# Sixteen rows of one V tile in layers two and four, moved from SP's queue to GpSimd's queue

## The chip, the cores and the metric

The kernel runs on one core of a Trainium2 chip. The metric is the device time of one launch in microseconds (us); the figure given for a version is the median of several runs. A profile of one execution, taken by the hardware profiler, goes with it. In what follows PE is the matrix engine (TensorE), DVE is VectorE, ACT is ScalarE, POOL is GpSimd, and SP is the engine that does little but issue DMAs. The core has 16 DMA engines, which do all transfers between HBM and the on-chip memory SBUF.

## The reference, cut to what matters

Four decode steps of attention, one token, one after the other; layers one and three use the weights and caches A, layers two and four B.

```python
def attention(x, k_cache, v_cache, wq, wo):        # x [1, 1, 640], caches [1, 32, 8192, 192]
    q = (x @ wq).reshape(1, 1, 32, 192).transpose(0, 2, 1, 3)
    scores = einsum("bhqd,bhkd->bhqk", q, k_cache) * 192 ** -0.5
    o = einsum("bhqk,bhkd->bhqd", softmax(scores), v_cache)
    return o.transpose(0, 2, 1, 3).reshape(1, 1, 32 * 192) @ wo

x = x + attention(layernorm(x), A_k, A_v, A_wq, A_wo)
x = x + attention(layernorm(x), B_k, B_v, B_wq, B_wo)
x = x + attention(layernorm(x), A_k, A_v, A_wq, A_wo)
x = x + attention(layernorm(x), B_k, B_v, B_wq, B_wo)
```

Everything is bf16. K and V of one layer are 2 x 32 x 8192 x 192 elements, so nearly all of the work is reading caches: the page of the profile counts 848 MB read in one launch.

## The kernel before

**Tiles.** The 32 heads are taken in 16 pairs. The K cache of a pair is one tile of 128 partitions: 64 partitions for each head, 128 keys of 192 elements on each, 49,152 bytes a partition. V of a pair has the same form. SBUF holds a `pool` of eight slots of half a tile (24,576 bytes a partition) each; a whole tile takes two neighbouring slots.

**One pair.** `products` (from line 589) multiplies K by the query on DVE in four chunks a half (line 599) and sums over the head dimension on PE with an identity matrix (lines 58 and 612). `softmax` takes maxima and exponentials. `values` (from line 641) multiplies the probabilities by V on PE (lines 58 and 678) and `gather` picks the two heads' results out of the accumulator (lines 696 and 697). At the end of a layer the last pair's results are projected by `wo` and give the next layer's input.

**Order of the work.** The program is written out by hand into one list of instructions for each engine (class `Queue`), with semaphores between them. `plan` is the list of transfers in the order in which SP issues them; `steps` is the order of the computation. `allot` gives each transfer of the plan its slots, and `before` names the tenants of those slots that must be done first. `transfer` (line 345) appends one DMA to SP's list behind waits for those tenants (`free`); `ahead` (line 404) appends as many as have known tenants. All 182 large transfers, the weights' too, go through SP's one queue, and each engine of the 16 takes its share of every transfer in that order. A tile whose halves are loaded together (`whole`) is one DMA of 128 rows of 49,152 bytes (line 379). Its completion adds 16 to the semaphore of its first slot, and `values` makes PE wait for that semaphore (line 664) before the first of its matmuls.

**Who else loads.** ACT issues one transfer, the 1.2 KB input `x` (line 420). The engines' own instructions come from HBM too, in pages, on queues of their own. POOL writes a few constants at the start and then does one small instruction in each layer (line 461, a power for the layer norm); it issues no DMA.

**Layers.** Layers one and two use index `l` 0 and 1, layers three and four 2 and 3; `p` counts the pairs of a layer in the order in which they are taken. The twelfth pair is `p` 11. Of the V tiles, pairs 14 and 15 of layer two stay in SBUF for layer four.

Of the kernel before, what the change touches and what calls it, by code (L numbers as in the profile page):

```python
# [7 lines left out]
BF16 = mybir.dt.bfloat16  # L8
# [53 lines left out]


PAIRS_W = 5
NSLOT = 8
KEPT = {0: {("k", 0)}, 1: {("v", 14), ("v", 15)}}


def build(nc, A_x, A_k, A_v, A_wq, A_wo, B_x, B_k, B_v, B_wq, B_wo, out):
    _, H, SK, DH = A_k.shape  # L70
    D = A_x.shape[-1]
    P = 128
# [9 lines left out]
    PD = 2 * DH  # L82
    NW = PAIRS_W * PD // P
    QC = (NPAIR - 1) * PD
    QR = QC // 3
    TS = JU * DH
# [5 lines left out]
    VK = 8  # L92
    FORWARD = dict(pairs=list(range(NPAIR)), q0=0, q1=1, wo=[0, PAIRS_W, 2 * PAIRS_W], wol=NPAIR - 1)
    BACKWARD = dict(pairs=[15, 14, 11, 12, 13] + list(range(1, 11)) + [0], q0=NPAIR - 1, q1=0,
                    wo=[NPAIR - PAIRS_W, 1, 1 + PAIRS_W], wol=0)
    ORDER = [FORWARD, FORWARD, FORWARD, BACKWARD]

    with ExitStack() as ctx:
        def sb(name, shape, dt):
            return ctx.enter_context(nc.sbuf_tensor(name, shape, dt))  # L100
# [4 lines left out]
        def sem(name):  # L105
            return ctx.enter_context(nc.semaphore(name))

        ident = sb("ident", [P, P], BF16)
        pool = sb("pool", [P, NSLOT * TS], BF16)
# [36 lines left out]
        xb = sb("xb", [P, DC], BF16)  # L146
        zero = sb("zero", [P, 33], BF16)
        part = [sb(f"part{i}", [P, DC], BF16) for i in range(3)]

        QM = ps("QM")  # L150
        SP_ = [ps("S0"), ps("S1")]
# [15 lines left out]
        PE = Queue(sem("pPE"))  # L167
        DV = Queue(sem("pDVE"))
        AC = Queue(sem("pACT"))
        PO = Queue(sem("pPOOL"))  # L170
        SP = Queue()
        semS = [sem(f"semS{i}") for i in range(NSLOT)]
        semOL, semOE, semOB, semVQ, semX, semOUT = [sem(n) for n in ("semOL", "semOE", "semOB", "semVQ", "semX", "semOUT")]

        e = PO.op(lambda g: g.memset(ident[:], 0.0))
        PO.op(lambda g: g.affine_select(out=ident[:], in_=ident[:], compare_op=ALU.not_equal, fill=1.0,
# [33 lines left out]
        def whole(kind, l, p):  # L210
# [3 lines left out]
            if kind == "k":  # L214
                return l < 2 and p not in (PAIRS_W, 2 * PAIRS_W) or l == 3 and p > 1
            if p == NPAIR - 1:
                return False
            return l != 2 or p not in (0, PAIRS_W, 2 * PAIRS_W)

# [6 lines left out]
        for l in range(NL):  # L226
# [8 lines left out]
            for p in range(NPAIR):  # L235
# [17 lines left out]
                if p < NPAIR - 2:  # L253
                    if first_load("v", l, p) == (l, p):
                        plan += [("v", l, p, u) for u in range(2)]
                        if l == 2 and p == 1:
                            i = plan.index(("k", l, 1, 0))
# [70 lines left out]
                    plan[i:i + 2] = [m, n]  # L328
                    turn[n[1:3]] = (1, 0)

        freed, landed = {}, {}
        issued = [0]

        def wq_rows(l, g):
# [10 lines left out]
        def transfer(n):  # L345
            l = n[1]
            o = ORDER[l]
            w = W[l % 2]
            free = [freed[b] for b in before[n]]
            if n[0] in ("wol", "woe"):  # L350
                r0 = o["wol"] * PD
                a, b = (0, OI) if l < 3 else (0, OI - 1) if n[0] == "wol" else (OI - 1, OI)
                return SP.op(lambda s: s.dma_start(
                    rows[:, a * D:b * D], w["wo"][r0:r0 + PD].rearrange("(p i) n -> p (i n)", p=P)[:, a * D:b * D]),
                    *free, sem=semOL if n[0] == "wol" else semOE, inc=16)
            if n[0] == "t":
                return max(free, key=lambda e: e[1]) if free else None
            if n[0] == "wob":
                r0 = o["wo"][2] * PD
                return SP.op(lambda s: s.dma_start(  # L360
                    slot[place[("wo", l, 2)]][:, (NW - NB[l]) * D:NW * D],
                    w["wo"][r0:r0 + PAIRS_W * PD].rearrange("(p i) n -> p (i n)", p=P)[:, (NW - NB[l]) * D:]),
                    sem=semOB, inc=16)
            if n[0] == "vq":
                n = ("v", l, NPAIR - 1, 1)
            i = place[n]
            t = slot[i]
            if n[0] in "kv":
                h = 2 * pair(l, n[2])
                r = w[n[0]][0, h:h + 2].rearrange("h (p j) d -> (h p) (j d)", j=J)  # L370
                if quarters(n):
                    x = TS // 2
                    if n in landed:
                        return SP.op(lambda s: s.dma_start(t[:, x:], r[:, TS + x:]), sem=semVQ, inc=16)
                    return SP.op(lambda s: s.dma_start(t[:, 0:x], r[:, TS:TS + x]), *free, sem=semS[i], inc=16)
                if whole(*n[:3]):
                    if n[3] == 1:
                        return landed[n[:3] + (0,)]
                    f = lambda s: s.dma_start(pool[:, i * TS:(i + 2) * TS], r)
                else:  # L380
                    f = lambda s: s.dma_start(t, r[:, n[3] * TS:(n[3] + 1) * TS])
            elif n[0] == "wq" and l < 2:
                f = lambda s: s.dma_start(pool[:, i * TS:i * TS + DC * QW], w["wq"].rearrange("(p c) n -> p (c n)", c=DC))
            elif n[0] == "wq":
                c0, k = Q_PARTS[n[2]]
                f = lambda s: s.dma_start(
                    wq_rows(l, n[2]),
                    w["wq"][:, o["q1"] * PD:o["q1"] * PD + QC].rearrange("(p c) n -> p c n", c=DC)[:, c0:c0 + k, :])
            else:
                r0 = o["wo"][n[2]] * PD  # L390
                k = NW - NB[l] if n[2] == 2 else NW
                f = lambda s: s.dma_start(
                    t[:, 0:k * D], w["wo"][r0:r0 + PAIRS_W * PD].rearrange("(p i) n -> p (i n)", p=P)[:, 0:k * D])
            return SP.op(f, *free, sem=semS[i], inc=16)

        def need(n):

            while n not in landed:
                m = plan[issued[0]]
                issued[0] += 1  # L400
                landed[m] = transfer(m)
            return landed[n]
# [45 lines left out]
        def layer(l, ev_z, ev_true):  # L448
# [192 lines left out]
            def values(p, us=(0, 1)):  # L641

                par = (l * NPAIR + p) % 2
                nl, np_ = first_load("v", l, p)
                k = 2 if p == NPAIR - 1 else VK
                N = min(512, k * DH)
                PE.wait(ev_p[p])
                if 0 in us:
                    PE.wait(last["rl"])
                    if p < NPAIR - 1:  # L650
                        e = PE.op(lambda t: t.matmul(TB[96:97, C_L:C_L + 2], lhsT=ones[:, 0:1], rhs=l_col[par][:],  # L651
                                                     start=True, stop=True), bank=TBu)
                    else:
                        for h in range(2):
                            e = PE.op(lambda t, h=h: t.matmul(TB[64 * h:64 * h + 64, C_L:C_L + 1], lhsT=ones[:, 0:1].broadcast_to([P, 64]),
                                                              rhs=l_col[par][:, h:h + 1], start=True, stop=True),
                                      signal=h == 1, bank=TBu)
                    last["lc"][par] = ev_l[p] = e
                PE.wait(last["O"])
                rounds = J // k // G  # L660
                for r in range(us[0] * rounds // 2, (us[-1] + 1) * rounds // 2):
                    u, i = divmod(r, rounds // 2)
                    u = turn[nl, np_][u]
                    PE.wait(need(("v", nl, np_, u)))
                    t = slot[place[("v", nl, np_, u)]]
                    if p == NPAIR - 1 and i == rounds // 4 and quarters(("v", nl, np_, u)):
                        if l == 3:
                            busy(6)
                        PE.wait(need(("vq", l)))
                    for c in range(k * DH // N):  # L670
                        for g in range(G):
                            j = (i * G + g) * k
                            o, x, y = (O[32 * g:32 * g + 2 * k, c * N:(c + 1) * N],
                                       p_sb[par][:, u * JU + j:u * JU + j + k, :].rearrange("p j h -> p (j h)"),
                                       t[:, j * DH + c * N:j * DH + (c + 1) * N])
                            f, fin = r == 0, r == rounds - 1
                            e = PE.op(lambda t, c=c, g=g, o=o, x=x, y=y, f=f, fin=fin: (
                                t.matmul(o, lhsT=x, rhs=y, start=f, stop=fin) if c == 0 else  # L678
                                matmul_held(t, o, x, y, f, fin, 32, 32 * g)),
                                signal=(fin and c == k * DH // N - 1 and g == G - 1), bank=Ou)  # L680
                if 1 not in us:
                    return
                ev_O[p] = last["p"][par] = e
                if not stays("v", l, p):
                    for u in range(2):
                        freed[("v", nl, np_, u)] = e
# [80 lines left out]
            if l + 1 == NL:  # L767
                a = slot[place[("wo", 3, 2)]][0:33, 0:HD]
# [63 lines left out]
```

## Time and profile before

| | us |
|---|---|
| median of 3 runs | 1982.47 |
| lowest, highest | 1982.34, 1984.11 |
| the profiled execution: first to last instruction (its span) | 1982.1 |

No other time is listed for the profiled execution. Its span is 0.4 us under the median, which is the launch around the span and the difference between executions.

| | |
|---|---|
| bytes read from HBM | 848.36 MB |
| mean rate over the span | 428 GB/s |
| busy: PE, DVE, ACT, POOL | 65%, 61%, 7%, under 1% |
| twelfth V tile of layer two: issued by SP, landed | 855.92, 888.5 |
| the same of layer four | 1809.76, 1855.1 |

The times of the last two rows are from the span's start. The trace records, besides the instructions, every packet that the DMA engines moved (its queue, start, duration and size, but not which engine moved it) and the time of each of the 16 steps by which a transfer's completion raises its semaphore, one for each DMA engine. One row of a K or V tile is one packet. Where such records are used, the text says so; everything else is on the page of the profile or in its views of waits, chain and timeline.

### The profile page before, as it was taken

The numbers are of one execution on the slowest core, as the hardware profiler recorded it, in microseconds if no ns is written. First come the engines' busy times: TensorE is split into PE (matmuls) and PEld (weight loads), VectorE is DVE, ScalarE is ACT, GpSimd is POOL, SyncE is SP. The second block draws the span as 40 slices with busy tenths as digits, with TensorE's granted clock in tenths as the row PEclk, the third lists the DMA queues.
The fourth block names the chain that finished last, engine by engine and source line by source line (L and its number), as shares of the span: only waits on it lengthen the run. The fifth ranks groups of instructions, "written<-read, shape, count | busy, mean of one in ns | idle before, by whom it ended". The sixth has DMA issues, their size and how long they took to land.

```text
span 1982.1 us, 13748 instructions
## 1 busy us (share of the span) xinstructions
PE 1288.6 (65%) x8248; PEld 146.4 (7%) x3160; DVE 1201.2 (61%) x1376; ACT 139.9 (7%) x462; POOL 4.5 (0%) x23
## 2 busy tenths in 40 slices
PE   3567476666466666666785676675776766657658
PEld 0001001000100100100020010010001001000001
DVE  3566467467166657556745565665764775665656
ACT  0000000000000000000010000000000100000000
POOL 0000000000000000000000000000000000000000
PEclk9787776778677777777887877878787888777779
DMA  9999999999999999999999999999999999999998
GB/s 414 438 431 430 431 436 432 430 430 429 435 432 433 434 430 432 429 435 433 426 407 426 425 426 426 432 430 431 434 429 427 435 431 433 433 432 431 433 433 367
DMA packets 26930, 849.25 MB, mean 428 GB/s; under 512 B 3058, under 2 KB 3188, under 8 KB 3828
## 3 DMA queue, kind: packets, MB, share of 16 engines
q1 hardware_dynamic: 26724, 848.38, 99.6%
q8 instruction: 45, 0.74, 0.2%
q14 instruction: 17, 0.14, 0.0%
q10 hardware_dynamic: 144, 0.00, 0.0%
HBM read 848.36 MB, written 0.00 MB: 428 GB/s over the span
## 4 chain that ended last, share of the span: by engine, by line
DMA 67%; DVE 17%; PE 15%; ACT 1%; issue 0%; SPq 0%
DMA pool<-in_B_k_cache_dram 27%; DMA pool<-in_A_v_cache_dram 20%; DVE pool L599 15%; DMA pool<-in_A_k_cache_dram 14%; PE S L58 6%; DMA pool<-in_B_v_cache_dram 6%; PE OY L58 5%; PE OY L678 3%; DVE acc L697 1%; ACT p_sb L636 1%; DVE s_sb L621 1%; PE S L612 0%; DVE m_bf L623 0%; PE OY L538 0%; PE QM L626 0%
## 5 line engine op out<-in xcount | busy, mean ns | idle before, releaser
L599 DVE TENSOR_TENSOR pool<-pool,q_sb 128x3072 bf16<-128x3072 bf16 x512 | 861.1, 1753 | 229.5 <-DMA pool<-in_B_k_cache_dram 133.5
L58 PE MATMUL S<-pool,ident 128*128 128x512 bf16 x2944 | 789.5, 425 | 19.5 <-DVE pool L599 17.6
L710 PE MATMUL TB<-acc,small 128*1 128x192 f32 x240 | 82.7, 495 | 212.0 <-DVE acc L697 212.0
L58 PE MATMUL OY<-pool,p_sb 128*16 128x512 bf16 x1920 | 202.7, 498 | 0.0
L696 DVE TENSOR_SCALAR acc<-OY,small 128x192 f32<-128x192 f32 x64 | 26.7, 418 | 287.5 <-PE OY L58 256.3
L678 PE MATMUL OY<-pool,p_sb 128*16 128x512 bf16 (+1 forms) x1216 | 148.2, 495 | 69.5 <-DMA pool<-in_A_v_cache_dram 63.5
L612 PE MATMUL S<-pool,ident 128*128 128x512 bf16 x128 | 61.8, 483 | 201.3 <-DVE pool L599 201.2
L697 DVE SCALAR_TENSOR_TENSOR acc<-OY,small,acc 128x192 f32<-128x192 f32 x424 | 177.1, 418 | 14.9
L621 DVE TENSOR_REDUCE s_sb<-S 128x64 f32<-128x512 f32 x128 | 88.0, 688 | 69.7 <-PE S L58 69.7
L527 ACT ACTIVATE q_sb<-QM 128x192 bf16<-128x192 f32 x60 | 19.9, 331 | 944.0 <-PE QM L521 944.0
L721 ACT ACTIVATE rows<-TB,small 1x192 bf16<-1x192 f32 x120 | 43.2, 406 | 596.3 <-PE TB L710 596.3
L692 DVE RECIPROCAL small<-TB 1x2 f32<-1x2 f32 x64 | 11.2, 175 | 94.5 <-PE TB L651 75.3
L636 ACT ACTIVATE p_sb<-s_sb,small 64x128 bf16<-64x128 f32 x128 | 55.7, 435 | 161.2 <-DVE small L630 160.4
L612 PEld LDWEIGHTS S<-pool,ident 128*128 128x128 bf16 x128 | 12.9, 101 | 676.2 <-DVE pool L599 604.4
L651 PE MATMUL TB<-small,ones 128*1 128x2 f32 x120 | 11.4, 165 | 74.1 <-ACT p_sb L636 74.1
L678 PEld LDWEIGHTS OY<-pool,p_sb 128*16 128x16 bf16 (+1 forms) x1216 | 39.8, 107 | 217.3 <-issue 138.8
L626 PE MATMUL QM<-ident,m_bf 128*64 128x64 bf16 x128 | 14.0, 216 | 54.4 <-DVE m_bf L623 53.9
L710 PEld LDWEIGHTS TB<-acc,small 128*1 128x1 f32 x240 | 19.8, 101 | 310.8 <-DVE acc L697 284.0
L630 DVE TENSOR_REDUCE small<-QM 128x1 f32<-128x64 f32 x64 | 14.4, 225 | 35.2 <-PE QM L626 35.2
L521 PEld LDWEIGHTS QM<-rows,one_b 1*64 1x64 bf16 x120 | 6.2, 100 | 347.0 <-issue 341.1
L538 PE MATMUL OY<-oT,pool 128*128 128x1 bf16 x675 | 28.6, 178 | 1.9 <-ACT oT L584 1.9
L538 PEld LDWEIGHTS OY<-oT,pool 128*128 128x128 bf16 x675 | 27.8, 131 | 3.8 <-ACT oT L584 2.5
(74 smaller groups left out, 215.2 us busy)
## 6 DMA issues: line engine op xcount, KB each, us to landing
pool<-in_B_k_cache_dram SPq DMA_DIRECT2D x28, 6144.0 KB, 37.9
pool<-in_B_v_cache_dram SPq DMA_DIRECT2D x28, 6144.0 KB, 33.5
pool<-in_A_v_cache_dram SPq DMA_DIRECT2D x27, 6144.0 KB, 27.5
pool<-in_A_k_cache_dram SPq DMA_DIRECT2D x34, 3072.0 KB, 20.5
pool<-in_A_k_cache_dram SPq DMA_DIRECT2D x14, 6144.0 KB, 36.4
pool<-in_A_v_cache_dram SPq DMA_DIRECT2D x10, 3072.0 KB, 14.7
pool<-in_B_k_cache_dram SPq DMA_DIRECT2D x8, 3072.0 KB, 22.5
pool<-in_A_wo_dram SPq DMA_DIRECT2D x6, 2400.0 KB, 21.9
```

The source lines that it names most:

```text
L58: return t.add_instruction(mybir.InstMatmult(name=t.bass.get_next_instruction_name(), engine=mybir.EngineType.PE, ins=[t.lower_ap(rhs), t. ...
L527: lambda a: a.activation(q_sb[i][:], QM[:, 0:DH], ACT.Copy), e, last["q"][i], bank=QMu)
L538: e = PE.op(lambda t, i=i, c=c, f=y_first[0], fin=n[0] == "wol" and i == k - 1: t.matmul(YB[:, c:c + 1], lhsT=t3[:, i, c:D:DC], rhs=o[:, i ...
L599: e = DV.op(lambda v, d0=d0: v.tensor_tensor(k3[:, :, d0:d0 + QD], kin[:, :, d0:d0 + QD], q_sb[qi][:, d0:d0 + QD].unsqueeze(1).broadcast_t ...
L612: t.matmul(S[:, :], lhsT=ident[:], rhs=k3[:, :, d0:d0 + R], start=True, stop=fin) if d0 == 0 else
L621: lambda v, u=u: v.tensor_reduce(s[:, u * JU:(u + 1) * JU], SP_[u][:].rearrange("p (j r) -> p j r", r=R), AX.X, ALU.add), ev_S[p, u], last ...
L636: ev_p[p] = AC.op(lambda a, h=h, r=r: a.activation(p_sb[par][r, :, h], s[r, :], ACT.Exp, bias=negm[par][r, 0:1], accum_out=l_col[par][r, h ...
L678: t.matmul(o, lhsT=x, rhs=y, start=f, stop=fin) if c == 0 else
L696: v.tensor_scalar(acc[:], O[:, 0:DH], pick[:, 0:1], None, ALU.mult) if i == 0 else
L697: v.scalar_tensor_tensor(out=acc[:], in0=O[:, i * DH:(i + 1) * DH], scalar=pick[:, i:i + 1], in1=acc[:], op0=ALU.mult, op1=ALU.add)), e if ...
L710: e = PE.op(lambda t, h=h: t.matmul(TB[96:97, C_O + h * DH:C_O + (h + 1) * DH], lhsT=half[:, h:h + 1], rhs=acc[:], start=True, stop=True), ...
L721: last["TO"] = last["row_written"] = AC.op(lambda a, h=h: a.activation(orow[:, o0 + h * DH:o0 + (h + 1) * DH], TB[96:97, C_O + h * DH:C_O ...
```

## The change

The V tile of the twelfth pair in layers two and four (`("v", 1, 11)` and `("v", 3, 11)`) comes in five transfers in place of one. SP issues the first 112 rows. POOL issues the last 16 in two transfers of eight rows, 112 to 119 and 120 to 127. Ahead of each of these it issues a transfer of the first two elements of the same eight rows (4 bytes a row) into a tile `turned` that nothing reads. All four wait, on POOL, for the same tenants as SP's transfer, and add 16 each to a new semaphore `semA`. PE waits for `semA` as well as for the slot's semaphore before the first matmul of that tile. The lists of DVE and ACT are as before; SP's has the same transfers in the same order, two of them with 112 rows in place of 128; POOL's gains eight DMAs, four behind its second small instruction (the one of layer two) and four behind its last.

```diff
+ASIDE = {("v", 1, 11), ("v", 3, 11)}
+ASIDE_ROWS = 16
...
+        turned = sb("turned", [P, 2], BF16)
...
-        freed, landed = {}, {}
+        freed, landed, aside = {}, {}, {}
...
                 if whole(*n[:3]):
                     if n[3] == 1:
                         return landed[n[:3] + (0,)]
-                    f = lambda s: s.dma_start(pool[:, i * TS:(i + 2) * TS], r)
+                    if n[:3] in ASIDE:
+                        for a in range(P - ASIDE_ROWS, P, 8):
+                            PO.op(lambda g, a=a: g.dma_start(turned[a:a + 8], r[a:a + 8, 0:2]), *free, sem=semA, inc=16)
+                            aside[n[:3]] = PO.op(lambda g, a=a: g.dma_start(pool[a:a + 8, i * TS:(i + 2) * TS], r[a:a + 8]),
+                                                 *free, sem=semA, inc=16)
+                        a = P - ASIDE_ROWS
+                        f = lambda s: s.dma_start(pool[0:a, i * TS:(i + 2) * TS], r[0:a])
+                    else:
+                        f = lambda s: s.dma_start(pool[:, i * TS:(i + 2) * TS], r)
...
-                    PE.wait(need(("v", nl, np_, u)))
+                    PE.wait(need(("v", nl, np_, u)), aside.get(("v", nl, np_)))
```

More of the change, by code (lines that the diff above doesn't have):

```diff
@@ L172, in build @@
         semS = [sem(f"semS{i}") for i in range(NSLOT)]
-        semOL, semOE, semOB, semVQ, semX, semOUT = [sem(n) for n in ("semOL", "semOE", "semOB", "semVQ", "semX", "semOUT")]
+        semOL, semOE, semOB, semVQ, semX, semOUT, semA = [
+            sem(n) for n in ("semOL", "semOE", "semOB", "semVQ", "semX", "semOUT", "semA")]
         e = PO.op(lambda g: g.memset(ident[:], 0.0))
```

## The prediction

> **What bounds the kernel now.** I read the slices first, then the table of queues.
>
> ```profile
> DMA  9999999999999999999999999999999999999998
> GB/s 414 438 431 430 431 436 432 430 430 429 435 432 433 434 430 432 429 435 433 426 407 426 425 426 426 432 430 431 434 429 427 435 431 433 433 432 431 433 433 367
> ...
> q1 hardware_dynamic: 26724, 848.38, 99.6%
> q8 instruction: 45, 0.74, 0.2%
> q14 instruction: 17, 0.14, 0.0%
> q10 hardware_dynamic: 144, 0.00, 0.0%
> ```
>
> The DMA engines are full in every slice; only the 21st (the change to layer three, 407) and the last (367) fall off. So the time is bytes over rate, and a gain or loss must come from how evenly the 16 engines are loaded. The page gives only their mean. The packet records give more: a row of 49,152 bytes takes 1.815 us, and each engine starts the next at once. Chaining packets (the one that starts where another ended) gives sixteen unbroken chains, one an engine. They start within 1.1 us of one another and drift apart. The 16 completion steps say the same: they lie 1.1 us apart for the first transfer and 6.35 us for layer two's last V transfer.
>
> What drives the drift is the other queues. Each 16,384-byte instruction page (q8) puts one engine back by 1.55 us, and these pages go round exactly eight engines in turn. Each 8,192-byte page of one kind (q14) puts back a ninth engine, always the same, by 0.97 us, six times before the end of layer two. The other seven are hardly hit. Lag behind the first engine:
>
> - end of layer two: seven at 0 to 1.82 us, the eight page engines at 2.95 to 5.67, the ninth at 6.35;
> - end of layer four: seven at 0 to 2.25, the eight at 3.18 to 6.18, the ninth at 5.36.
>
> The chain of work that ended last shows that the slowest engine is the one that counts, and at just these two ends:
>
> ```profile
> 993.05 16.54 DMA pool<-in_B_v_cache_dram
> 1009.62 1.48 PE OY L678 x14
> ...
> 1937.43 37.95 DMA pool<-in_B_v_cache_dram
> 1975.43 0.85 PE OY L678 x16
> ```
>
> PE starts on the layer's last V piece 0.04 us after it has landed whole. In between the queue never runs dry, so the lags are carried on; at the change to layer three the fast engines do run dry (the spread falls to 2.4 us), so layer two's lag is paid, and layer four starts its own.
>
> **The change, part by part.**
>
> *SP's transfers.* Two of 128 rows become 112: seven rows an engine in place of eight, if all 16 share evenly as in every transfer of the trace. Each engine is relieved of 1.815 us a layer.
>
> *POOL's eight-row transfers.* A row is one packet in all K and V transfers shown, so eight rows reach at most eight engines. Each transfer has a small one of the same row count ahead of it; if the seats are given out in turn, small ones sit on one eight and large ones on the other, both times. Then eight engines carry 7 + 2 = 9 rows (1.82 us more than before) and eight carry 7 (1.82 less). No row of this trace shows which eight. But there are nine late engines and eight seats, and the nine are split: whichever eight is loaded, somebody late is in it.
>
> - If the loaded eight are those without q8 pages, they hold the ninth engine: layer two ends at 6.35 + 1.82 = 8.17 (+1.82), layer four at 5.36 + 1.82 = 7.18 against 6.18 (+1.00). Sum +2.8.
> - If the loaded eight are the page engines: 5.67 + 1.82 = 7.49 against 6.35 (+1.14), and 6.18 + 1.82 = 8.00 (+1.82). Sum +3.0.
> - The best eight (the seven quick ones and the least late): 2.95 + 1.82 = 4.77 against 6.35 (-1.58), 3.18 + 1.82 = 5.00 against 6.18 (-1.18). Sum -2.8.
>
> I take the mean of the first two, +2.9, because the pages' eight look like a half of the engines, as the seats would be; the third needs a set drawn for this purpose.
>
> [...]
>
> *Cost of a second queue beside the first.* No POOL DMA is in the trace. The nearest rows: the 10-byte packets of ACT's one transfer (q10) put the rows beside them back by nothing that shows; a 16,384-byte page costs 1.55 us, where its size at a row's rate is 0.60, so 0.95 too much; an 8,192-byte page 0.97 against 0.30, so 0.67. Between 0 and 0.95 I take 0.5 a large packet, near the middle, since a row is data like q1's but its queue is software-fed like neither. Two packets a loaded engine and layer: 4 x 0.5 = +2.0 (0 to 3.8). Nothing excludes that it is below that of q1's own rows, but an engine that is never idle has nothing to win.
>
> *The small transfers and completions.* Eight packets of 4 bytes each, and 16 completion steps for each of four transfers. Completion packets on q1 take 9 ns: 4 x 9 ns is nothing. From above, the smallest page's 0.67 for each of four on every engine: 2.7 a layer, 5.4 in all. I take 0, the nearer in size.
>
> *POOL's list.* Four waits and four issues a layer. Behind the first four stands line 461 of layer three, and for that there is time:
>
> ```profile
> 855.92 0.33 SPq L379 DMA_DIRECT2D pool<-in_B_v_cache_dram  x1
> ...
> 1016.75 0.55 POOL L461 TENSOR_TENSOR small<-small 128x1 f32<-128x1 f32 x1 [501.41 <-DVE small L460]
> ```
>
> POOL waits for the same tenants as SP, so it is let go by 855.92 and has 160 us before its next instruction. Nothing stands behind the second four. Price: 0; if POOL were late there, ACT's scaling of the query waits for it.
>
> *PE's added wait.* Behind it stands PE's whole list: the V products, then the next pair's sums. SP's part of the tile lands at 888.5, 32.6 us after its issue, because some 18 us of other transfers (32.6 less its own 8 x 1.815) are ahead of it on q1; in layer four it is 45 us. POOL's rows have their own queue and need two rows' time, 2 x 1.815, or twice that when they alternate with q1's. Even behind the whole backlog they come with SP's rows. Price: 0; if they took longer, each us past 888.5 + 3.2 (PE takes the tile up at 891.7) is a us of PE, of which the backlog on q1 hides the first 18.
>
> *SP and DVE, ACT.* SP issues the same number of DMAs (0.33 us each); DVE and ACT have the same lists. 0.
>
> **The sum.** Span 1982.1 + 2.9 + 2.0 = 1987.0, and 0.4 around it (median of the runs less the span): **1987.4**. This case alone reaches from 1982.1 + 0.4 + 2.8 = 1985.3 to 1982.5 + 3.0 + 3.8 + 5.4 = 1994.7.
>
> **The rivals.**
>
> 1. *The balance improves.* The seats fall on the quick engines and relieve the late ones: -2.8, and with no second-queue cost 1979.7. For it: the spread of 6.35 us is real, and the mean of the lags at the two ends is some 3 us, so there is something to win. Against it: nine late for eight seats. It decides from the point where the loaded eight hold at most one late engine.
> 2. *The change doesn't move the load.* If the two large transfers sit on different eights, every engine carries 7 + 1 = 8 rows as before, and only a second-queue packet remains, one an engine and layer: 2 x 0.5 = +1.0, so 1983.5. Speaks for it that nothing shows the seats' order.
> 3. *The rows of the side transfers hinder one another.* Eight neighbouring partitions are filled by eight engines at once, which no transfer of the trace does. From above: one after the other, 8 x 1.815 = 14.5 us a transfer, 29.0 a layer against the 3.6 in my sum, so +25 a layer, up to 2038. It counts only as far as a loaded engine's q1 rows stand still meanwhile; a page shows that they do, the row beside it takes 0.48 us longer on top of the page's 1.07. Against it: every row of the trace took 1.82 with 16 engines writing at once. I put it at a third of that, 2004.
>
> [...]
>
> **How the numbers follow.** My forecast's case has 0.52, rival 1 0.09, rival 2 0.14, rival 3 0.20, and 0.05 is for what I don't see (POOL's transfers late). The range runs from rival 1 (1979.5) to the end of the forecast's case (1995) and leaves out rival 3 and little else. A measurement of this kernel can tell about 0.2% from no change, 4.0 us: below 1978.5, above 1986.4. Faster beyond that: 0.04, since the balance can't give it. Slower: rival 3, three fifths of the forecast's case, most of the unseen: 0.57. Within: 0.39.
>
> **What would show it.** On the page: two new queues' worth of packets beside q1, 32 rows fewer on q1. In the completion steps of layer two's last V transfer: a spread of over 7.5 us shows the load on late engines, under 5 rival 1, about 6.5 rival 2, over 12 rival 3. The side rows' own packets: about 1.8 us each, or 4 and more for rival 3. The forecast is wrong if the loaded eight are the quick ones, if the side rows take much longer than q1's, or if PE waits for `semA` where it waited for the slot (line 664 of before).

## The result

The changed kernel took **2055.32 us** (median of 4 runs, 2053.57 to 2059.34), the kernel before 1982.4 on the same chip (4 runs, 1981.95 to 1984.11). The ratio is 1.037, with a 95% interval of 1.0356 to 1.0384: 72.9 us slower, against 5 foretold and a range that ended at 1995. The profiled execution took 2055.56, its span is 2053.7.

**The profile after.** The slices and the table of queues, from the page:

```profile
DMA  9999999999999999999999999999999999999998
GB/s 414 433 435 431 430 430 433 435 429 430 434 430 432 430 436 428 376 213 428 425 392 430 427 429 433 434 417 436 426 427 436 430 431 434 435 430 254 333 433 340
...
q1 hardware_dynamic: 26692, 846.80, 98.8%
q0 software_dynamic: 256, 1.57, 0.6%
q8 instruction: 45, 0.74, 0.1%
```

The two rows must be read together. The first still says 9 in every slice but the last, as before; the second falls to 213 GB/s in the 18th slice and to 254 in the 37th. These are the places of the two changed tiles. The DMA engines were busy there, but at half the rate: a packet that is held up counts as busy (below, from 870 to 885 us, a share of 1.03 at 206 GB/s). POOL's q0 moved 1.57 MB, 0.2% of the bytes.

The same stretch of layer two in windows, after and then before (columns: stretch, its length, the busy time and count of PE, PE's weight loads, DVE, ACT and POOL, the PE clock, the DMA share, GB/s):

```profile
850.00:870.00 20.00, 12.87 (x84) 1.25 (x27) 7.11 (x15) 1.31 (x5) 2.24 (x4) 0.79 1.14 335
870.00:885.00 15.00, 0.00 (x0) 0.00 (x0) 0.00 (x0) 0.72 (x2) 0.00 (x0) 0.50 1.03 206
885.00:925.00 40.00, 14.63 (x66) 0.68 (x16) 15.42 (x13) 1.31 (x5) 0.00 (x0) 0.63 0.93 208
925.00:945.00 20.00, 10.60 (x63) 0.82 (x17) 9.98 (x12) 0.72 (x2) 0.00 (x0) 0.62 1.00 433
```

```profile
850.00:870.00 20.00, 13.02 (x86) 1.22 (x27) 7.06 (x15) 1.54 (x6) 0.00 (x0) 0.80 1.00 431
870.00:885.00 15.00, 8.97 (x34) 0.20 (x2) 10.95 (x7) 0.49 (x2) 0.00 (x0) 0.70 1.00 433
885.00:925.00 40.00, 26.15 (x176) 2.13 (x50) 24.57 (x32) 3.34 (x12) 0.00 (x0) 0.83 1.00 432
925.00:945.00 20.00, 12.03 (x45) 0.54 (x6) 14.83 (x13) 0.72 (x2) 0.00 (x0) 0.74 1.01 435
```

From 870 to 925 the rate is 206 to 208; before, the same four stretches had 431 to 435. From 870 to 885 PE and DVE do nothing at all: they have run out of tiles. The rate comes back at once after the tile (433 from 925 to 945).

How long the transfers took (columns: tile, engine that issues, count, KB of each, median us from issue to landing), the two kinds of the change, and the whole V tiles of B before:

```profile
pool<-in_B_v_cache_dram SPq DMA_DIRECT2D x2, 5376.0 KB, 76.4
...
pool<-in_B_v_cache_dram POOLq DMA_DIRECT2D x4, 384.0 KB, 28.4
```

```profile
pool<-in_B_v_cache_dram SPq DMA_DIRECT2D x28, 6144.0 KB, 33.5
```

SP's 112 rows needed 76.4 us (such a tile of 128 rows before: 33.5), POOL's eight rows 28.4. The chain of work that ended last, in the places that the prediction showed and in the one where the time went:

```profile
850.42 48.39 DMA pool<-in_B_k_cache_dram
...
916.64 7.42 another core or an unknown queue
...
1021.83 15.84 DMA pool<-in_B_v_cache_dram
...
2009.17 37.75 DMA pool<-in_B_v_cache_dram
```

The K tile issued at 850.42, just ahead of the changed V tile, already took 48.4 us. Before, the same tile was issued at 850.79 and by its completion steps had landed at 874.0, after 23.2 us, so rows of a transfer that was not changed are slow too. At 916.64 PE waits 7.42 us for the changed tile. The view cannot name the queue. The completion steps can: `semA` had its last step at 898.5 us from the span's start, and SP's 112 rows theirs at 924.06, where PE's wait ends. So PE waited for SP's rows, not for POOL's. The pieces at 1021.83 and 2009.17 stand at the ends of layers two and four. The second is the same last V piece as before, 37.75 us against 37.95. The first is the half tile just ahead of layer two's last two V pieces, 15.84 us; before, the chain went through the last of these, 16.54. They are no longer than the pieces before; they start later. By the completion steps, layer two's last V transfer lands 35.4 us later than before, layer four's 71.5: **some 36 us a layer**.

**The packet records.** Of layer two's 49,152-byte rows on q1 between the start of the stretch and 100 us later:

```
kernel   rows over 2.4 us   median of these   longest   they span
before          0                 -             2.3         -
after         214               3.67            8.5      61.4 us
```

POOL's sixteen rows took 6.2 to 8.4 us (the first eight) and 3.9 to 6.8 (the second). Nothing but the two tiles' transfers was changed, so what remains is to find what makes their rows slow.

### The profile page after: what moved, and what is told of

It reads as the page before. It is cut to its first block, busy times and chain, and to the rows that moved or that the text cites. A ratio compares the mean times of both kernels' runs of the same rounds, so it can differ in the third digit from the quotient of the medians.

```text
span 2053.7 us, 13758 instructions
## 1 busy us (share of the span) xinstructions
PE 1291.0 (63%) x8248; PEld 146.3 (7%) x3160; DVE 1201.1 (58%) x1376; ACT 139.8 (7%) x462; POOL 8.8 (0%) x31
## 3 DMA queue, kind: packets, MB, share of 16 engines
q0 software_dynamic: 256, 1.57, 0.6%
## 4 chain that ended last, share of the span: by engine, by line
DMA 63%; PE 18%; DVE 15%; another core or an unknown queue 3%; ACT 1%; issue 1%; SPq 0%
DMA pool<-in_B_k_cache_dram 24%; DMA pool<-in_A_v_cache_dram 21%; DMA pool<-in_A_k_cache_dram 13%; DVE pool L611 12%; PE S L58 8%; PE OY L58 5%; DMA pool<-in_B_v_cache_dram 4%; PE OY L690 3%; DVE acc L709 1%; ACT p_sb L648 1%; DMA pool<-in_A_wq_dram 1%; DVE s_sb L633 1%; PE S L624 0%; PE OY L550 0%
## 5 line engine op out<-in xcount | busy, mean ns | idle before, releaser
L642 DVE TENSOR_REDUCE small<-QM 128x1 f32<-128x64 f32 x64 | 14.4, 225 | 35.4 <-PE QM L638 35.4
```

## The experiments

All are made from the changed kernel by replacing the block under `if n[:3] in ASIDE:`; only the two V tiles differ from one to the next. `f` is SP's last transfer, `sp` and `po` stand for a DMA on SP's or POOL's list, `D[a:b]` and `r[a:b]` for those rows of the slot and the cache, `semA` is used as in the change. Where a median stands without an interval it is one execution. "A layer" is half of the difference from the kernel before. The theory of the landing places, in the expectations, is that rows in flight together slow one another by the partitions into which they go; it was a conjecture of mine, and no run had shown how the partitions are grouped.

### Which of the five transfers is it?

**sp_112_16**: SP issues the 16 rows too, POOL none.

```diff
-  po(turned[a:a+8], r[a:a+8, 0:2]); po(D[a:a+8], r[a:a+8])    # a = 112, 120
-  f = sp(D[0:112], r[0:112])
+  sp(D[0:112], r[0:112]); f = sp(D[112:128], r[112:128])
```

> Nothing goes by GpSimd's queue: SP issues the 112 rows and then the 16 rows of both tiles. [...] Theory of GpSimd's queue (its packets block the engines): 1982, rows at 1.82. Theory of load alone (my forecast): 1982.

Measured 2027.48: +45, 22.5 a layer, without POOL. q1's rows take 3.5 to 3.8 us during the 112 rows and up to 6.2 during the 16. So most of the loss needs neither POOL nor its queue.

**pool_128**: POOL carries both tiles whole, SP nothing of them.

```diff
+  return po(D[0:128], r[0:128])
```

> Both tiles come whole, 128 rows, by GpSimd's queue, nothing of them by SP. [...] Theory of GpSimd's queue: eight packets on each of 16 engines in place of two on eight, so more than the changed kernel lost, over 2055. Load alone: 1982.

Measured 1985.78 (1985.39 to 1987.77), ratio 1.0019, interval 1.0009 to 1.0028. GpSimd's queue beside SP's costs 3.3 us for 256 rows, where the change gives it 32. Its rows took a median of 1.82 us. The theory of a costly second queue falls.

**no_small**: as the change, without the two small transfers.

```diff
-  po(turned[a:a+8], r[a:a+8, 0:2])
```

> The changed kernel without the small transfers ahead of the eight-row ones. [...] Theory of GpSimd's queue: each of its packets costs the engine some 17 us in the changed kernel (35 us a layer over two), so one an engine gives some +35, 2017. Load alone: 1982 to 1984. If the time stays at 2055, the small transfers did nothing for the seats.

Measured 2058.93: as the change, and a miss. I had thought that without the small ones the two eight-row transfers would sit on different eights. They don't: as far as the packets can be chained, the same eight engines carry two side rows each in both kernels.

**small_only**: the small transfers alone, SP's tile whole.

```diff
-  po(D[a:a+8], r[a:a+8]);  f = sp(D[0:112], r[0:112])
+  f = sp(D[0:128], r[0:128])
```

> Only the small transfers of 8 x 4 bytes go by GpSimd's queue, SP loads both tiles whole. Landing places: no change, 1981 to 1984. Theory of GpSimd's queue in the form that waking it or its completions cost: up to 2055. Load alone: 1982 to 1983.

Measured 1982.49, ratio 1.0 (0.9991 to 1.0009). They cost nothing.

### Source, size and number

**sp_src7**: 128 rows as before, but read from rows of the cache that begin 43,008 bytes apart in place of 49,152 (seven eighths, as 112 is of 128).

```diff
+  r7 = AP(r.tensor, r.offset, [[7*2*TS//8, 128], [1, 2*TS]]);  f = sp(D[0:128], r7)
```

> [...] Landing places: nothing changes, 1981 to 1984, rows at 1.82 us. Source theory (the engines meet in HBM, since each begins seven rows behind the next in place of eight): as the 112 rows in a line did, 2010 to 2027, rows at 3.6 us.

Measured 1982.41, ratio 1.0 (0.9991 to 1.001). It reads other data than the reference's; its time tells that this distance between the rows that are read is not the cause.

**sp_cols8**: eight transfers of all 128 rows, an eighth of the columns each, as many and as large as those of **sp_16x8**: eight transfers of 16 neighbouring rows. **sp_64_64**: two of 64.

```diff
+  sp_cols8:  sp(D[:, c], r[:, c])            # c = eight column ranges, the last is f
+  sp_16x8:   sp(D[a:a+16], r[a:a+16])        # a = 0, 16, ... 112
+  sp_64_64:  sp(D[0:64], r[0:64]); f = sp(D[64:128], r[64:128])
```

> [...] Landing places: no change, 1981 to 1986. Theory of the small transfer: as the eight of 16 rows.

> SP loads both tiles as eight transfers of 16 rows, one row an engine. [...] Source theory: 1982 to 1990. [...]

> SP loads both tiles as two transfers of 64 rows, four rows an engine. [...] Source theory: each engine reads its rows in a line as before, 1982 to 1986.

Measured: sp_cols8 1983.53 (ratio 1.0005, 0.9995 to 1.0014), sp_16x8 2040.0 (28.7 a layer), sp_64_64 2025.41 (21.4 a layer). Eight transfers are free if each goes to all 128 partitions; the same bytes in eight transfers of 16 rows are not. So neither the number nor the size of the transfers is the cause; what differs is which partitions (and rows) one transfer takes. The slow rows of sp_16x8 in layer two have a median of 4.0 us. Why two halves cost 21.4 and eight times 16 rows no more than 28.7, the runs do not show.

### Fewer rows, or where they land?

Three theories stand against each other from here on, all conjectures of mine. A: rows in flight together slow one another by where they land. B: every transfer of fewer than 128 rows is slow. C: a landing place is eight neighbouring partitions.

**sp_even_odd** has two transfers of 64 rows like sp_64_64, the even partitions and the odd ones. **sp_step8** has eight of 16 rows like sp_16x8, with rows eight apart.

```diff
+  sp_even_odd:  sp(D[0:128:2], r[0:128:2]); f = sp(D[1:128:2], r[1:128:2])
+  sp_step8:     sp(D[a:128:8], r[a:128:8])   # a = 0 ... 7, the last is f
```

> SP sends both tiles as two 64-row transfers, the even partitions and then the odd ones. [...] Theory B (fewer than 128 rows): 2025. [...]

> SP sends both tiles as eight 16-row transfers with rows eight partitions apart (a, a+8, ... a+120). Against eight transfers of 16 neighbouring rows (2040.0) only the landing places differ. [...] Theory B: 2040. Theory C: 1982 to 1986.

Measured: sp_even_odd 1982.65, ratio 1.0 (0.9991 to 1.0009), with no slow rows (one of 2.5 us in layer four, as before); sp_step8 2022.92, ratio 1.0204 (1.0189 to 1.0219), with slow rows of a median of 3.7. The slices of sp_64_64 and of sp_even_odd, the same two transfers of 64 rows into other partitions:

```profile
GB/s 416 433 432 429 434 433 430 430 432 432 433 435 432 431 431 432 432 255 432 427 409 433 425 429 437 427 422 438 427 431 429 435 432 432 433 432 357 328 432 364
```

```profile
GB/s 413 434 434 430 430 430 433 435 431 428 437 429 432 430 435 431 428 433 435 426 409 426 429 431 430 434 430 426 434 430 428 432 434 434 431 431 431 436 429 367
```

The dips to 255 and 328 are gone in the second. "Fewer than 128 rows is slow" falls. None of the three theories as I had put them held both results: A had expected sp_even_odd to be slow, because I gave each engine four neighbouring rows of the list. Its core, that rows suffer by where they land, stays; how a transfer's rows are dealt out to the engines, no run shows. C had sp_step8 free.

**pool_8home** and **pool_8rows**: POOL carries both tiles in sixteen transfers of 8 rows, four apart or neighbouring.

```diff
+  pool_8home:  po(D[a:a+29:4], r[a:a+29:4])  # a = 0, 64, 1, 65, 2, 66, 3, 67, 32, 96, ...
+  pool_8rows:  po(D[a:a+8], r[a:a+8])        # a = 0, 8, ... 120
```

> GpSimd's queue carries the whole of both tiles as sixteen 8-row transfers, each with rows four partitions apart (0, 4, ... 28, then 64, 68, ... 92, and so on). [...] Theory B, any transfer of fewer than 128 rows is slow: as the contiguous one of this call, 2025 to 2045. Theory C, a place is eight neighbouring partitions: two engines share a place, 2012 to 2026.

> The same sixteen 8-row transfers by GpSimd's queue, but each into eight neighbouring partitions. Same number, size and queue as its twin; only the landing places differ. [...] Theory B: the same as its twin. Theory C: eight engines on one place: over 2080.

Measured: pool_8home 2071.19 (2065.46 to 2074.22), pool_8rows 2182.66 (2179.86 to 2185.2). pool_8rows lies where C had it, whose figures for sp_step8 and pool_8home fell. pool_8home is the most telling run of all in its rows. Each eight q0 rows in the order in which they ran, shortest, median and longest in us:

```
                        pool_8home           pool_8rows
1st transfer (0, 4, ... 28)    1.82 1.82 1.83    (0 to 7)    5.20 6.14 6.66
2nd transfer (64, 68, ... 92)  3.14 3.52 3.63    (8 to 15)   5.19 6.25 6.60
3rd transfer (1, 5, ... 29)    1.82 1.82 1.82    (16 to 23)  5.01 6.22 6.60
4th transfer (65, 69, ... 93)  3.14 3.48 3.56    (24 to 31)  5.12 5.77 6.71
```

As far as the packets can be chained, all q0 rows of pool_8home ran on the same eight engines. So one queue, one row count, one size and the same engines: into partitions 0 to 31, four apart, a row takes its 1.82 us; into 64 to 95 it takes twice that, and packed into eight neighbours three to four times. In the first case the eight engines hinder nobody: q1's rows that start beside the first transfer take 1.82 to 2.3 us, beside the second up to 3.63.

The later transfers of the same run show what the slow rows need. The even ones all go into 64 to 127. In layer two the 2nd, 4th, 6th and 10th have medians of 3.4 to 3.6 us, with 11 to 13 of q1's rows in flight on average; the 8th, 12th, 14th and 16th run at 1.81, with 7, 5, 2 and 1. In layer four the even ones up to the 14th take 3.4 to 3.6 (11 to 13 in flight), the 16th 1.81 (4). The odd ones, into 0 to 63, have medians of 1.81 to 2.0 with however many beside them. So the place alone does not make a row slow; rows of SP's queue must be in flight as well. What the rows share there, no run shows: the trace names neither engine nor place. That the kernel is slow all the same is, as I read it, because all 128 rows of a tile went through eight engines, and a part of them at half speed.

### The rule tried, and the loss split

**sp_step4** and **pool_32** have rows four apart, spread over all 128 partitions. In pool_32 POOL carries 32 of them, twice the side load of the change.

```diff
+  sp_step4:  sp(D[a:128:4], r[a:128:4])      # a = 0 ... 3, the last is f
+  pool_32:   aside = po(D[2:128:4], r[2:128:4]); sp(D[0:128:4], r[0:128:4]); f = sp(D[1:128:2], r[1:128:2])
```

> SP sends both tiles as four 32-row transfers, rows four partitions apart. Theory A (an engine loses time only where it writes into another engine's landing place; rows spread evenly over the partitions keep each engine at home, as the even and odd halves did): 1982 to 1985. Rival (the fewer rows a transfer has, the slower; two 64-row halves were just wide enough): between the 64-row transfers (1982.7) and the 16-row ones eight apart (2022.9), 1995 to 2015.

> A side load of the change's kind with spread rows: GpSimd's queue carries the 32 rows 2, 6, ... 126, SP the 32 rows 0, 4, ... 124 and the 64 odd ones. Theory A: nothing is shared, and a whole tile by GpSimd cost +3.3, so 1982 to 1986. Rival (a side transfer of fewer than 128 rows hinders SP's rows wherever it lands): 2010 to 2055.

Measured: sp_step4 1982.1, ratio 0.9998 (0.9989 to 1.0007); pool_32 1982.5, ratio 1.0 (0.999 to 1.0009). Slices, queues and issues of pool_32:

```profile
GB/s 413 436 434 431 429 432 430 438 429 428 437 431 429 432 436 433 427 433 434 424 413 431 427 430 432 430 428 429 432 430 427 436 432 432 434 432 431 433 433 367
q1 hardware_dynamic: 26692, 845.23, 99.3%
q0 software_dynamic: 96, 3.15, 0.4%
...
pool<-in_B_v_cache_dram POOLq DMA_DIRECT2D x2, 1536.0 KB, 13.5
```

q0 moves twice the bytes that it did in the change, no slice dips, and 32 rows land 13.5 us after the issue, where eight rows took 28.4. All of q0's rows took 1.81 to 2.3 us.

**sp_112_only** leaves out the last 16 rows of the two tiles, **pool_16_only** the first 112.

```diff
+  sp_112_only:   f = sp(D[0:112], r[0:112])
+  pool_16_only:  po(D[112:120], r[112:120]); po(D[120:128], r[120:128])
```

> SP's 112 neighbouring rows alone; the last 16 rows of the tile are left out. If the loss of 112 + 16 rows (+22.5 a layer) comes from the 112: half a row's rate for 7 rows and for the K rows around them, less one row of 1.8 us that is gone: 2008 to 2020. If the 16 rows make it: 1979 to 1984.

> GpSimd's two 8-row transfers alone; SP's 112 rows of the tile are left out, which takes 7 rows of 1.815 us, 12.7 us a layer, from every engine (1957 if nothing else happened). [...] If a side row goes at a row's own 1.8 us: 1961 to 1965.

Measured: sp_112_only 2013.26 (ratio 1.0153, 1.0138 to 1.0168), pool_16_only 1994.2 (1.0056, 1.0039 to 1.0073). Slices of the two, in this order:

```profile
GB/s 415 430 436 428 434 435 427 436 434 426 433 435 431 431 435 430 431 282 435 425 408 431 429 429 437 428 428 435 427 431 428 435 431 434 432 431 388 328 432 371
```

```profile
GB/s 414 434 429 437 429 435 430 429 436 424 438 428 434 433 429 434 431 281 373 429 422 427 432 430 432 431 430 430 432 430 427 437 428 435 431 431 306 432 431 358
```

Each alone dips at both tiles. Against the work that is left out:

- SP's 112 rows: +30.8 and two rows of 1.815 saved, 34.4 for two layers, **17.2 a layer**;
- POOL's 16 rows: 1982.46 less 7 rows of 1.815 in two layers is 1957.05; 1994.2 is 37.2 above it, **18.6 a layer**.

Together 35.8 a layer, 71.6 in all, against 72.9 measured for the change. The two halves of the change cost about the same, and they add up.

## Why the prediction was wrong

By its own steps:

- **What bounds the kernel**: right. It is DMA-bound before and after, and so a loss of rate goes into the time almost in full: in layer two, 20 us at 335 and 55 at about 207 in place of 432 GB/s lose 33 us, and the layers lost 35.4 and 36.1. A small thing in the sum: around the span lie 1.9 us (2055.56 and 2053.7), not 0.4; the sum starts from the measured time either way.
- **SP's transfers: this step failed first.** It gave the 112-row transfer seven rows an engine at 1.815 us, "if all 16 share evenly as in every transfer of the trace", and so a saving. Every transfer of that trace had 128 rows; the 112 were a shape that it did not show, and I bounded only POOL's. Measured: 3.6 us a row, K rows around it as well, 17.2 a layer in place of -1.8.
- **POOL's eight-row transfers**: the same eight engines did carry both, as the prediction said, but not for its reason, that small transfers take the seats between: they do so in no_small too. That was luck. And it gave a row 1.815 us; they took 3.9 to 8.4, and slowed K rows beside them. 18.6 a layer (pool_16_only) against +2.9 for both. The uneven load is there, small: the spread of completion steps behind the tile is 9.2 us, where it was 5.5 before, and at layer four's last V transfer 10.0 against 6.1; 3.7 to 3.9 more is about the 2 x 1.82 between eight engines with nine rows and eight with seven.
- **A second queue**: 0.5 us a packet was too much. pool_128 shows 3.3 us for 16 packets on each engine, 0.2 each (0.1 to 0.35 by its interval), and pool_32 nothing.
- **The small transfers**: 0, right (small_only).
- **POOL's list**: 0, right. Its DMAs go out early and the next instruction comes 194 us later:

```profile
855.83 0.71 POOL L385 DMA_DIRECT2D turned<-in_B_v_cache_dram  x1 [340.24 <-PE QM L533]
856.53 0.52 POOL L386 DMA_DIRECT2D pool<-in_B_v_cache_dram  x1
857.04 0.52 POOL L385 DMA_DIRECT2D turned<-in_B_v_cache_dram  x1
857.55 0.52 POOL L386 DMA_DIRECT2D pool<-in_B_v_cache_dram  x1
1052.19 0.56 POOL L473 TENSOR_TENSOR small<-small 128x1 f32<-128x1 f32 x1 [194.12 <-DVE small L472]
```

- **PE's added wait**: 0, right, but by luck. `semA` was complete at 898.5, later than the 888.5 + 3.2 of the prediction; that cost nothing only because SP's own rows came still later, at 924.06.

**The rivals.** The third, that the side rows hinder one another, had the mechanism for POOL's part: its sign of "4 and more" us a side row came true, that of a spread over 12 at layer two's last V transfer did not (6.6; three transfers earlier it still was 10.2, but the first engine was done with that one at 1020.2 and SP issued the next only at 1021.83, so the fast engines had run dry). It was priced at a third of 25 a layer, because every row of the trace took 1.82 us with 16 engines at work. That evidence was of one shape only. And it counted POOL's rows alone; nothing in the prediction let the rows of SP's own split transfer suffer. Chances and direction leaned the right way (0.57 for slower), the range could not hold it.

The runs sort by where the rows land. Free were rows one in two or one in four over all 128 partitions (sp_even_odd 1982.65, sp_step4 1982.1, pool_32 1982.5), slow were neighbouring rows (sp_64_64 2025.41, sp_16x8 2040.0) and rows one in eight (sp_step8 2022.92). K and V tiles came in transfers of 128 rows alone in the profile before, so the prediction had no row time for any such part.

**What stays open.** How the 112 rows are dealt out to the engines: the trace names neither a packet's row nor its engine, and they run at half rate (3.6 us) like those of two halves (3.73). And why the slow stretch is longer than the slow rows ask for: sp_64_64's 8 rows an engine at twice 1.815 us make 29 us, 14.5 lost, while its slow rows (median 3.73) span 42.7 us in layer two and cost 21.4 a layer. The completion steps of the K tile ahead lie 11.7 us apart there, 5.5 before, so engines ahead and behind may hinder each other across tiles; that is only argued. Last, in the splits by rows, a row's place in the cache and its partition change together; sp_src7 alone moves the one without the other, for one distance. That the partition decides there rests on that run and on pool_8home's transfers into 64 to 127, which were slow only with q1's rows beside them.

## What to carry to other kernels

In a stream that fills the DMA engines, splitting a tile along its partitions is not neutral (sp_64_64 lost 21.4 us a layer, sp_even_odd nothing): check where each part's rows land, and not only how many bytes each engine gets. If a tile must be split, split it along the columns with all 128 partitions in each part, or give each part every second or every fourth partition; those splits cost nothing that could be measured here (ratios of 1.0005, 1.0 and 0.9998 for sp_cols8, sp_even_odd and sp_step4). A row time from a trace holds for the shape that the trace shows; a shape that it lacks needs bounds of its own, on the queue that keeps most of the work too.

## What the runs showed of the hardware

- Rows of two transfers in flight can slow one another by where they land: from the same eight engines, 1.82 us into partitions 0 to 31 four apart, 3.5 into 64 to 95 while q1's rows run beside them, 1.81 again into that half when few do (pool_8home), and 4 to 8.4 into eight neighbours; a rate of 206 to 208 GB/s in place of 432 for the whole core. What the rows share is not shown.
- The busy share of the DMA engines does not show it (in the changed kernel 9 in tenths in every slice but the last, as before); the GB/s row does (213 and 254 in the slices of the two tiles).
- GpSimd's transfers of eight rows ran on the same eight engines each time (two in a row, or sixteen), as far as packets can be chained. In no_small, where no small transfer stands between the two, they did so too.
- A tile by GpSimd's queue cost 1.7 us more than by SP's (pool_128: 3.3 for two), and the 32 spread rows of pool_32 landed in 13.5 us: they need not stand behind SP's backlog, and in layer two the first of them started 3.8 us after POOL's issue.
